# Last inverse transform step on four quarters of TensorE's array, with a radix-2 step over s1, in a kernel of a 2-D spectral filter and a dense MLP

## The chip, the cores and the metric

One core of a Trainium2 chip runs the kernel alone. The metric is device time in microseconds (us) of one execution; lower is better. The engines are TensorE (PE; its weight loads are PEld), VectorE (DVE), ScalarE (ACT), GpSimd (POOL) and SyncE (SP). SP does nothing here but issue DMAs, one after the other, from one queue.

## What is computed

The reference, cut to what matters; x is 2048 tokens of 512 numbers, F is 1792:

```python
def _A_ref(x, w_r, w_i):                 # spectral filter
    X = rfft2(x); X = X * (w_r + 1j * w_i)
    return irfft2(X, (S, D))
def _B_ref(x, w1, b1, w2):               # dense -> mish -> dense
    h = einsum("bsd,df->bsf", x, w1) + b1
    return einsum("bsf,fd->bsd", h * tanh(softplus(h)), w2)
xn = layernorm(x)
out = x + _A_ref(xn, w_r, w_i) + _B_ref(xn, w1, b1, w2)
```

## The kernel before

**Numbers.** Every f32 operand of a matmul is split into a high and a low f16 part, and each product is three matmuls: high x high, high x low, low x high. `mm3` (L85) does such a triple; its three calls are L88, L91 and L92.

**The MLP.** Tokens form four groups g of 512, F forms 14 slices f of 128. A *half tile* is either `mlp_up(g, f)` (L771; twelve matmuls into `ph`, then on ScalarE a Mish and on ScalarE and VectorE the split of its result into `a`) or `mlp_down(g, f)` (twelve matmuls into four accumulators `pa`). Both are 128x128 weights by 128x512. There are 112 half tiles; the generator `mlp_all` (L856) hands them out one by one, and `half_tile` takes the next. The tokens of a group lie as columns of `xnT[g]`; `turn` and `copies` (L328) fill it. At the end of a group `mlp_end` (L845) adds the accumulators onto the rows `macc`, which by then hold x plus the spectral part; only group 3 does it in the other order: the spectral part comes first, and `mlp_end` stores the result.

**The transforms.** The token number is 16 s1 + s2. Forward: over s1 (`s1_forward`), over s2 with a first step over d (`p2_unit`, tile `psP`), over d (`d_pair`, `psD`); the product with the filter (`spectrum`); back over d (`dp_unit`, `psA`), over s2 (`ip_unit`, `psT`), and over s1 (`s1_inverse`, L886, `psY`). Between the steps the data go through HBM to be turned: `d_y1`, `d_a` and `d_t`. So an `ip_unit` reads its rows `ai` from `d_a`, makes six matmuls, and its result goes over ScalarE (`bc_t`), VectorE (`bt_t`), ScalarE (the cast to `tt`) and GpSimd (the low part of `tt`) to `d_t`. `s1_inverse` reads `yi` from `d_t`, in 512-byte pieces, once all sixteen `ip_unit`s have stored. `p2_unit` runs pairs of matmuls that use half of the array's columns each, `d_pair` pairs that use half of its rows each.

**The order.** From L1122 on the spectral work (`stream_a`, 120.6 units of weight, N_WGT) is mixed with half tiles so that at its end `B_END` = 98 of the 112 are given out. Then sixteen `s1_inverse` calls, one for each s2, are spread over the remaining 14: call k comes (k + T_LAG)(112 - T_HOLD - 98)/16 half tiles later, the first after three, and two half tiles are kept for the end. A scheduler turns this into an order for each engine; it may move the matmuls of half tiles past those of `s1_inverse`, of which only the first of three is held in place.

```python
def s1_inverse(g, s):
    s2 = 4 * g + s
    yi = qp.tile([P, 4, 2, P], F16, tag="q1", name=f"yi_{s2}")       # 4 buffers, shared with ai and yt
    ...
    psf = ps_f.tile([P, D], F32, tag="f", name=f"psY_{s2}")          # 2 buffers, shared with psP ... psT
    ...
    nc.vector.scalar_tensor_tensor(m, psf, sc["k"], m, op0=ALU.mult, op1=ALU.add)
    nc.sync.dma_start(outv[:, s2, :], m)
```

Of the kernel before, what the change touches and what calls it, by code (L numbers as in the profile page):

```python
# [19 lines left out]
P = 128  # L20
NS2 = 16
# [10 lines left out]
B_END = 98  # L32
T_LAG = 4
T_HOLD = 2
# [7 lines left out]
def spectral_mlp_kernel(ctx, tc, x, wt, w0, w1, b1, w2, cT, cIT, cM, out):  # L42
# [16 lines left out]
    outv = out.rearrange("(p s) d -> p s d", s=NS2)  # L59
# [179 lines left out]

    def turn(pt, xh, h):  # L240
        for dc in range(4):
            nc.tensor.transpose(pt[:, h, dc, :], xh[:, h, dc * P : (dc + 1) * P], ident)
# [10 lines left out]
    def first_group(ts):  # L253

        pe, act, dve = mybir.EngineType.PE, mybir.EngineType.Activation, mybir.EngineType.DVE
        with in_order(pe, act, dve):
# [4 lines left out]
            xTv = xnT[0].rearrange("p h c (s t) -> p h c s t", s=4)  # L261
# [26 lines left out]
            def copy(s):  # L288
                nc.vector.tensor_copy(xTv[:, 0, :, s, :], pt[s][:, 0])
                return nc.scalar.copy(xTv[:, 1, :, s, :], pt[s][:, 1])  # L290
# [33 lines left out]
    def turned_rows(g, s, xh):  # L324
# [6 lines left out]
        def copies():  # L331
            xTv = xnT[g].rearrange("p h c (s t) -> p h c s t", s=4)
            nc.vector.tensor_copy(xTv[:, 0, :, s, :], pt[:, 0])
            nc.scalar.copy(xTv[:, 1, :, s, :], pt[:, 1])  # L334
# [409 lines left out]
    def ip_unit(c, g):  # L744
# [4 lines left out]
        for k in range(2):  # L749
# [12 lines left out]
        nc.sync.dma_start(  # L762
            d_t.rearrange("a (c f) e -> (a c) (f e)", c=2)[:, fg * 1024 : (fg + 1) * 1024],
            tt.rearrange("p l h e -> p (l h e)"),
        )
# [116 lines left out]
    def load_it():  # L882
        t = cp.tile([P, NS2, 2, P], F16, tag="cT", name="cITt")
# [3 lines left out]
    def s1_inverse(g, s):  # L887
        s2 = 4 * g + s
        yi = qp.tile([P, 4, 2, P], F16, tag="q1", name=f"yi_{s2}")
        nc.sync.dma_start(  # L890
            yi.rearrange("p a h e -> p a (h e)"),
            d_t[4 * s2 : 4 * s2 + 4].rearrange("a p e -> p a e"),
        )
        psf = ps_f.tile([P, D], F32, tag="f", name=f"psY_{s2}")
        yv = yi.rearrange("p a h (b e) -> p h b a e", b=2)
        mm3(
            psf.rearrange("p (b a e) -> p b a e", b=2, a=4),
            lambda h: sc["cIT"][:, s2, h, :],
            lambda h: yv[:, h],
            True,  # L900
            True,
            True,
        )
        if g < 3:
            m = macc[g][:, s, :]
            nc.vector.scalar_tensor_tensor(m, psf, sc["k"], m, op0=ALU.mult, op1=ALU.add)  # L906
# [373 lines left out]
```

## Time and profile before

| | |
|---|---|
| three runs | 400.53, 398.08, 399.92 us; median 399.92 |
| the profiled execution | 398.09 us, of which the trace spans 396.3 |
| TensorE busy | 379.8 us of the span, 2481 matmuls |
| VectorE, ScalarE, GpSimd busy | 241.2, 210.3, 68.9 us |
| DMA | 61.6 MB, mean 155 GB/s |
| granted TensorE clock | 1.00 |

The trace's times are microseconds from its start. A row of a group gives busy time in us, then the mean duration of one in ns. A matmul's duration contains its way through the array (a 128x512 one lasts 0.38 us), but one follows the other sooner; how fast matmuls go is read from the distance of their starts. In brackets stands how long an engine stood idle before an instruction, and what ended the wait.

### The profile page before, as it was taken

How to read it: one execution, taken by the hardware profiler on the slowest of the kernel's cores; microseconds unless marked ns; L12 is line 12 of the kernel's file. 1: busy time of each engine (PE TensorE's matmuls, PEld its weight loads, DVE VectorE, ACT ScalarE, POOL GpSimd, SP SyncE). 2: the span in 40 equal slices, each digit the busy share in tenths (PEclk: the TensorE clock that was granted, in tenths of full speed). 3: DMA queues.
4: the chain of work that ended last, by engine and by line, in shares of the span. 5: the costliest groups of instructions: out<-in, count | busy, mean ns of one | idle time of the engine just before them, and what ended most of it. 6: DMA issues, size and time to landing. Idle time of an engine off the chain costs nothing. (4 is left out here: it accounts for less than half of the span.)

```text
span 396.3 us, 6567 instructions
## 1 busy us (share of the span) xinstructions
PE 379.8 (96%) x2481; PEld 190.7 (48%) x2481; DVE 241.2 (61%) x505; ACT 210.3 (53%) x337; POOL 68.9 (17%) x100
## 2 busy tenths in 40 slices
PE   8799897999999999999999999999999999999995
PEld 3444343455544445456444565454655456444442
DVE  5789773465566724984597644957349972424334
ACT  3869858478665426564644555366455464423110
POOL 0000018366644400000021100121001120220000
PEclk9999999999999999999999999999999999999999
DMA  8995014335157894055732636226652022744556
GB/s 286 372 402 244 1 55 132 108 126 168 53 160 217 237 276 127 0 134 131 242 108 80 163 105 180 91 104 159 216 160 80 27 81 73 218 151 135 172 194 253
DMA packets 49519, 61.61 MB, mean 155 GB/s; under 512 B 3776, under 2 KB 36032, under 8 KB 48848
## 3 DMA queue, kind: packets, MB, share of 16 engines
q1 hardware_dynamic: 49488, 61.20, 49.1%
q8 instruction: 19, 0.31, 0.3%
q14 instruction: 12, 0.10, 0.1%
HBM read 44.38 MB, written 16.78 MB: 154 GB/s over the span
## 5 line engine op out<-in xcount | busy, mean ns | idle before, releaser
L781 PE MATMUL ph<-xnT,w1t 128*128 128x512 f16 x672 | 153.4, 379 | 1.3 <-ACT xnT L334 0.8
L781 PEld LDWEIGHTS <-w1t 128*128 128x128 f16 x672 | 65.0, 98 | 78.6 <-issue 1.5
L91 PE MATMUL pa<-w2r,a 128*128 128x512 f16 x224 | 84.9, 379 | 2.9 <-DVE w2r L499 1.9
L88 PE MATMUL pa<-w2r,a 128*128 128x512 f16 x224 | 85.0, 379 | 0.8 <-ACT w2r L496 0.5
L92 PE MATMUL pa<-w2r,a 128*128 128x512 f16 x224 | 84.9, 379 | 0.0
L795 ACT ACTIVATE hb<-ph,b1t,sc_exp 128x512 f32<-128x512 f32 x56 | 43.2, 772 | 56.1 <-PE ph L781 56.0
L816 DVE SCALAR_TENSOR_TENSOR a<-hb,sc_a,a 128x512 f16<-128x512 f32 x56 | 41.8, 750 | 51.0 <-ACT a L813 50.7
L133 POOL TENSOR_TENSOR tt<-bt_t,tt 128x512 f16<-128x512 f32 x16 | 19.9, 1245 | 186.3 <-ACT tt L132 186.3
L813 ACT ACTIVATE a<-hb,sc_a 128x512 f16<-128x512 f32 x56 | 40.1, 720 | 1.5
L92 PEld LDWEIGHTS <-a 128*128 128x128 f16 x224 | 21.9, 98 | 29.1 <-issue 3.7
L91 PEld LDWEIGHTS <-a 128*128 128x128 f16 x224 | 21.9, 98 | 25.5 <-issue 1.9
L88 PEld LDWEIGHTS <-a 128*128 128x128 f16 x224 | 21.9, 98 | 25.2 <-issue 0.8
L379 ACT ACTIVATE u<-r,sc_u 128x512 f16<-128x512 f32 x16 | 11.5, 720 | 23.6 <-DVE r L679 15.5
L133 POOL TENSOR_TENSOR y<-bt_s,y 128x512 f16<-128x512 f32 x16 | 18.7, 1177 | 10.8 <-issue 6.0
L132 ACT CAST tt<-bt_t 128x512 f16<-128x512 f32 x16 | 9.9, 616 | 15.9 <-DVE bt_t L128 12.5
L906 DVE SCALAR_TENSOR_TENSOR m<-psY,sc_k,m 128x512 f32<-128x512 f32 x12 | 8.7, 746 | 14.9 <-PE psY L92 14.9
L237 POOL TENSOR_TENSOR xh<-xs,xh 128x512 f16<-128x512 f32 x12 | 14.5, 1210 | 10.3 <-ACT xh L236 10.3
L734 DVE SCALAR_TENSOR_TENSOR at<-psA,at 128x512 f16<-128x512 f32 x16 | 10.7, 687 | 8.7 <-ACT at L733 8.7
L611 ACT ACTIVATE ix<-psD 64x512 f32<-64x512 f32 x16 | 9.5, 594 | 11.2 <-PE psD L599 10.9
L132 ACT CAST y<-bt_s 128x512 f16<-128x512 f32 x16 | 9.9, 616 | 10.4 <-DVE bt_s L128 7.6
L588 DVE SCALAR_TENSOR_TENSOR z<-psP,z 128x512 f16<-128x512 f32 x16 | 10.5, 684 | 7.8 <-ACT z L587 7.8
L127 DVE SCALAR_TENSOR_TENSOR bt_s<-psS,bc_s 128x256 f32<-128x256 f32 x16 | 6.7, 422 | 13.1 <-ACT bc_s L123 9.5
(158 smaller groups left out, 512.7 us busy)
## 6 DMA issues: line engine op xcount, KB each, us to landing
wt<-in_wt_dram SPq DMA_DIRECT2D x32, 256.0 KB
x<-in_x_dram SPq DMA_DIRECT2D x8, 512.0 KB
d_y<-y SPq DMA_DIRECT2D x16, 256.0 KB
wm<-in_wt_dram SPq DMA_DIRECT2D x8, 512.0 KB
yt<-d_y SPq DMA_DIRECT2D x16, 256.0 KB
d_a<-at SPq DMA_DIRECT2D x32, 128.0 KB
ai<-d_a SPq DMA_DIRECT2D x16, 256.0 KB
d_t<-tt SPq DMA_DIRECT2D x16, 256.0 KB
```

Of the source, the lines that this page charges most:

```text
L88: first = nc.tensor.matmul(ps, stat(0), mov(0), start=start, stop=False)
L91: nc.tensor.matmul(ps, stat(0), mov(1), start=False, stop=False)
L92: return nc.tensor.matmul(ps, stat(1), mov(0), start=False, stop=stop)
L132: nc.scalar.copy(out[:, :, 0, :], tv)
L133: nc.gpsimd.tensor_sub(out[:, :, 1, :], tv, out[:, :, 0, :])
L237: nc.gpsimd.tensor_sub(xh[:, 1, :], xs, xh[:, 0, :])
L379: hi = nc.scalar.activation(dst_h, src, AF.Copy, scale=scale)
L734: nc.vector.scalar_tensor_tensor(at[:, :, 1, :], psv, 2.0**-15, at[:, :, 0, :], op0=ALU.mult, op1=ALU.subtract)
L781: last_mm = nc.tensor.matmul(ph, w1t[:, hs, dc, f * P : (f + 1) * P], xnT[g][:, hm, dc, :], start=n == 0, stop=n == 11)
L795: nc.scalar.activation(hb, ph, AF.Mish, bias=b1t[:, f : f + 1], scale=s_exp[k])
L813: hi = nc.scalar.activation(a[:, 0, :], hb, AF.Copy, scale=sc["a"])
L816: lo = nc.vector.scalar_tensor_tensor(a[:, 1, :], hb, sc["a"], a[:, 0, :], op0=ALU.mult, op1=ALU.subtract)
```

## The change

The inverse over s1 is a sum over 64 frequencies f1, real and imaginary: 128 rows. Split by the parity of f1 (`be`), 64 rows each, the sum over even f1 is the same for s1 and s1 + 64, and that over odd f1 has the other sign. So for one s2 it is enough to compute 64 outputs t from the even rows and 64 from the odd rows, and then even + odd and even - odd. Each of these is a matmul of 64 rows by 64 columns of weights, a quarter of the array: row half by parity, column half (`i`) by which of two s2 of a pair. One call of the new `s1_inverse(g, q)` does two s2, 4g + q and 4g + 2 + q: twelve matmuls 64*64 by 512 into two PSUM tiles, even and odd, where two old calls made six 128*128 by 512.

What follows from it: the odd tile is copied by ScalarE (`odd`), VectorE does two multiply-adds from the even tile and one add, GpSimd one subtraction. Output rows now come as 64 t by i; so the columns of `xnT` are written in that order (`columns`), the residual rows are loaded and the results stored by 64 partitions, group 3's stores from SP's and ScalarE's queue. The rows of `d_t` are sorted by parity, so `tt` is stored by two DMAs. The turned rows of a pair are loaded one call ahead (`load_yi`); a call's stores are issued before the next call but after its loads. The order of TensorE in this stage is fixed as written (`in_order`). B_END is 97, T_LAG and T_HOLD are 3, and the last call is three half tiles before the end. The constants of this step (cIT) are half as large. The diff's core:

```diff
-B_END = 98
-T_LAG = 4
-T_HOLD = 2
+B_END = 97
+T_LAG = 3
+T_HOLD = 3
...
+    def columns(xT):
+        v = xT.rearrange("p h c (w q i t) -> p h c q i w t", w=2, q=2, i=2)
+        return [v[:, :, :, s % 2, s // 2] for s in range(4)]
...
         def copies():
-            xTv = xnT[g].rearrange("p h c (s t) -> p h c s t", s=4)
-            nc.vector.tensor_copy(xTv[:, 0, :, s, :], pt[:, 0])
-            nc.scalar.copy(xTv[:, 1, :, s, :], pt[:, 1])
+            xTv = columns(xnT[g])
+            pv = pt.rearrange("p h c (w t) -> p h c w t", w=2)
+            nc.vector.tensor_copy(xTv[s][:, 0], pv[:, 0])
+            nc.scalar.copy(xTv[s][:, 1], pv[:, 1])
...
-        nc.sync.dma_start(
-            d_t.rearrange("a (c f) e -> (a c) (f e)", c=2)[:, fg * 1024 : (fg + 1) * 1024],
-            tt.rearrange("p l h e -> p (l h e)"),
-        )
+        rows = d_t.rearrange("a (b c f) e -> b a c (f e)", b=2, c=2)
+        for be in range(2):
+            nc.sync.dma_start(
+                rows[be, :, :, fg * 512 : (fg + 1) * 512],
+                tt[:, 2 * be : 2 * be + 2].rearrange("p l h e -> p (l h e)"),
+            )
...
     def rows_back(g):
         macc[g] = cp.tile([P, 4, D], F32, tag=f"xnT{g}", name=f"m_{g}")
-        nc.sync.dma_start(macc[g], xv[:, 4 * g : 4 * g + 4, :])
+        for i in range(2):
+            nc.sync.dma_start(
+                macc[g][64 * i : 64 * i + 64].rearrange("t (w q) d -> t w q d", w=2),
+                xp[:, :, 4 * g + 2 * i : 4 * g + 2 * i + 2],
+            )
...
-                nc.sync.dma_start(outv[:, 4 * g + s, :], m[:, s, :])
+                for i, eng in enumerate((nc.sync, nc.scalar)):
+                    eng.dma_start(outp[:, s // 2, 4 * g + 2 * i + s % 2], m[64 * i : 64 * i + 64, s, :])
...
     def load_it():
-        t = cp.tile([P, NS2, 2, P], F16, tag="cT", name="cITt")
+        t = cp.tile([P, NS2, 2, 64], F16, tag="cT", name="cITt")
         nc.sync.dma_start(t, cIT.rearrange("p (s h q) -> p s h q", s=NS2, h=2))
         sc["cIT"] = t
-    def s1_inverse(g, s):
-        s2 = 4 * g + s
-        yi = qp.tile([P, 4, 2, P], F16, tag="q1", name=f"yi_{s2}")
-        nc.sync.dma_start(
-            yi.rearrange("p a h e -> p a (h e)"),
-            d_t[4 * s2 : 4 * s2 + 4].rearrange("a p e -> p a e"),
-        )
-        psf = ps_f.tile([P, D], F32, tag="f", name=f"psY_{s2}")
-        yv = yi.rearrange("p a h (b e) -> p h b a e", b=2)
-        mm3(
-            psf.rearrange("p (b a e) -> p b a e", b=2, a=4),
-            lambda h: sc["cIT"][:, s2, h, :],
-            lambda h: yv[:, h],
-            True,
-            True,
-            True,
-        )
+    def load_y(q):
+        y = sc["y", q] = big.tile([P, 2, D], F32, tag="big", name=f"y_{q}")
+        for i in range(2):
+            nc.sync.dma_start(y[64 * i : 64 * i + 64], xp[:, :, 12 + 2 * i + q])
+    yi_of, to_store = {}, []
+    def load_yi(g, q):
+        yis = []
+        for i in range(2):
+            s2 = 4 * g + 2 * i + q
+            yi = qp.tile([P, 4, 2, P], F16, tag="q1", name=f"yi_{s2}")
+            nc.sync.dma_start(
+                yi.rearrange("p a h e -> p a (h e)"),
+                d_t[4 * s2 : 4 * s2 + 4].rearrange("a p e -> p a e"),
+            )
+            yis.append(yi.rearrange("p a h (b e) -> p h b a e", b=2))
+        yi_of[g, q] = yis
+    def store_rows():
+        while to_store:
+            g, q = to_store.pop(0)
+            mv = macc[g].rearrange("p (w q) d -> p w q d", w=2)
+            for i in range(2):
+                nc.sync.dma_start(outp[:, :, 4 * g + 2 * i + q], mv[64 * i : 64 * i + 64, :, q])
+    def s1_inverse(g, q):
+        yis = yi_of.pop((g, q))
+        ps = [ps_f.tile([P, D], F32, tag="f", name=f"psY_{g}_{q}_{be}") for be in range(2)]
+        for t, (hs, hm) in enumerate(((0, 0), (0, 1), (1, 0))):
+            for i in range(2):
+                for be in (1, 0):
+                    rows = slice(64 * be, 64 * be + 64)
+                    mm = nc.tensor.matmul(
+                        ps[be][64 * i : 64 * i + 64].rearrange("p (b a e) -> p b a e", b=2, a=4),
+                        sc["cIT"][rows, 4 * g + 2 * i + q, hs, :],
+                        yis[i][rows, hm],
+                        start=t == 0,
+                        stop=t == 2,
+                    )
+                    tc.keep_in_program_order(mm)
+        odd = tp.tile([P, D], F32, tag="bt", name=f"odd_{g}_{q}", bufs=2)
+        nc.scalar.activation(odd, ps[1], AF.Copy, scale=sc["k"])
         if g < 3:
-            m = macc[g][:, s, :]
-            nc.vector.scalar_tensor_tensor(m, psf, sc["k"], m, op0=ALU.mult, op1=ALU.add)
-            nc.sync.dma_start(outv[:, s2, :], m)
+            ms = [macc[g][:, 2 * w + q, :] for w in range(2)]
         else:
-            if s % 2 == 0:
-                sc["y"] = big.tile([P, 2, D], F32, tag="big", name=f"y_{s2}")
-                nc.sync.dma_start(sc["y"], xv[:, s2 : s2 + 2, :])
-            y = sc["y"][:, s % 2, :]
-            nc.vector.scalar_tensor_tensor(y, psf, sc["k"], y, op0=ALU.mult, op1=ALU.add)
-            yacc.setdefault(g, []).append(y)
+            ms = [sc["y", q][:, w, :] for w in range(2)]
+            yacc.setdefault(g, {}).update({2 * w + q: ms[w] for w in range(2)})
+        for w in range(2):
+            nc.vector.scalar_tensor_tensor(ms[w], ps[0], sc["k"], ms[w], op0=ALU.mult, op1=ALU.add)
+        nc.vector.tensor_add(ms[0], ms[0], odd)
+        nc.gpsimd.tensor_sub(ms[1], ms[1], odd)
+        if g < 3:
+            to_store.append((g, q))
...
-    todo = [(3, s) for s in range(4)] + [(g, s) for g in range(3) for s in range(4)]
+    load_y(0)
+    load_y(1)
+    todo = [(3, q) for q in range(2)] + [(g, q) for g in range(3) for q in range(2)]
+    load_yi(*todo[0])
     start, n = done[0], len(todo)
     total = 2 * 4 * NFC
-    for k in range(n):
-        while done[0] - start < (k + T_LAG) * (total - T_HOLD - start) / n and half_tile():
+    with in_order(mybir.EngineType.PE):
+        for k in range(n):
+            while done[0] - start < T_LAG + k * (total - T_HOLD - T_LAG - start) / (n - 1) and half_tile():
+                pass
+            if k + 1 < n:
+                load_yi(*todo[1])
+            store_rows()
+            s1_inverse(*todo.pop(0))
+        store_rows()
+        while half_tile():
             pass
-        s1_inverse(*todo.pop(0))
...
-    order = (np.arange(2)[:, None] * 64 + np.arange(64).reshape(16, 2, 2).transpose(0, 2, 1).reshape(1, 64)).reshape(128)
-    IT = T.transpose(2, 1, 0)[order]
+    order = (np.arange(2).reshape(1, 2, 1, 1) * 64 + np.arange(64).reshape(16, 2, 2).transpose(2, 0, 1)[:, None]).reshape(128)
+    IT = T.transpose(2, 1, 0)[order][:, :, :64]
```

How the change moves instructions, at four places. In these rows L is the line in the file that the row is from; `ph_3_8` is `mlp_up` of group 3, slice 8, `pa` is `mlp_down`, `psT_15` the last `ip_unit`, and the number after that a tile's own. "..." leaves out the rest of such a group of matmuls and their weight loads.

TensorE, before, from the last `ip_unit` to the first last-step matmul (psY):

```order
L88 MATMUL psT_15_4117<-ai_15_4115,cMt_88 128x256
...
L88 MATMUL pa_3_3_3740<-w2r_93,a_3_5_3858 128x512
...
L781 MATMUL ph_3_9_4145<-xnT_3_1251,w1t_92 128x512
...
L88 MATMUL pa_3_0_3737<-w2r_93,a_3_6_3926 128x512
...
L781 MATMUL ph_3_10_4184<-xnT_3_1251,w1t_92 128x512
...
L88 MATMUL psY_12_4177<-yi_12_4175,cITt_1367 128x512
...
```

TensorE, after, the same place:

```order
L90 MATMUL psT_15_4117<-ai_15_4115,cMt_88 128x256
...
L792 MATMUL ph_3_8_4144<-xnT_3_1252,w1t_92 128x512
...
L90 MATMUL pa_3_0_3769<-w2r_93,a_3_5_3891 128x512
...
L792 MATMUL ph_3_9_4174<-xnT_3_1252,w1t_92 128x512
...
L939 MATMUL psY_3_0_1_4197<-yi_12_4140,cITt_1368 64x512
...
L939 MATMUL psY_3_0_0_4196<-yi_12_4140,cITt_1368 64x512
...
L939 MATMUL psY_3_0_1_4197<-yi_14_4142,cITt_1368 64x512
...
```

Between psT_15 and psY stood 3 + 12 + 12 + 8 = 35 full matmuls, now 5 + 12 + 12 = 29. The third psY matmul needs a second turned row, yi_14. At the end of the program TensorE's last work was six psY matmuls and is now 36 of `pa`.

ScalarE, before, in the last `ip_unit`s:

```order
L795 ACTIVATE hb_3_8_4110<-ph_3_8_4097,b1t_94,sc_exp_1_317 128x512
L813 ACTIVATE a_3_8_4112<-hb_3_8_4110,sc_a_327 128x512
L123 ACTIVATE bc_t_14_4089<-psT_14_4081 128x256
L132 CAST tt_14_4088<-bt_t_14_4091 128x4x128
L123 ACTIVATE bc_t_15_4125<-psT_15_4117 128x256
L132 CAST tt_15_4124<-bt_t_15_4127 128x4x128
```

ScalarE, after:

```order
L125 ACTIVATE bc_t_13_4075<-psT_13_4067 128x256
L125 ACTIVATE bc_t_14_4106<-psT_14_4098 128x256
L134 CAST tt_13_4074<-bt_t_13_4077 128x4x128
L134 CAST tt_14_4105<-bt_t_14_4108 128x4x128
L125 ACTIVATE bc_t_15_4125<-psT_15_4117 128x256
L806 ACTIVATE hb_3_8_4157<-ph_3_8_4144,b1t_94,sc_exp_1_317 128x512
L134 CAST tt_15_4124<-bt_t_15_4127 128x4x128
L824 ACTIVATE a_3_8_4159<-hb_3_8_4157,sc_a_327 128x512
```

The last unit's first copy now stands behind the casts of two other units, and hb_3_8 has moved ahead of its cast. On TensorE these units, too, stand closer: psT_13 and psT_14 without a matmul between them, three full ones before psT_15.

SP, after, the DMAs of the last four `ip_unit`s and the first `yi`:

```order
L748 DMA d_a_86<-at_13_3975 64x4x256 x2
L756 DMA ai_12_4046<-d_a_86 128x2x512
L748 DMA d_a_86<-at_14_4005 64x4x256 x2
L748 DMA d_a_86<-at_15_4023 64x4x256 x2
L756 DMA ai_13_4065<-d_a_86 128x2x512
L756 DMA ai_14_4096<-d_a_86 128x2x512
L756 DMA ai_15_4115<-d_a_86 128x2x512
L773 DMA d_t_87<-tt_12_4055 64x2x512 x2
L773 DMA d_t_87<-tt_13_4074 64x2x512 x2
L773 DMA d_t_87<-tt_14_4105 64x2x512 x2
L773 DMA d_t_87<-tt_15_4124 64x2x512 x2
L916 DMA yi_12_4140<-d_t_87 128x4x256
```

Before, ai_13 was issued ahead of the stores of at_14 and at_15, and ai_15 only after the store of tt_12. The first psT_12 has 14 full matmuls between it and the last psA, before it had ten.

In the spectral stream before that the new pace moves half tiles about: before the very first psT, 45 full matmuls follow the last psA (22 before), and at two places where twelve full matmuls stood between two pairs of psP units only two are left.

More of the change, by code (lines that the diff above doesn't have):

```diff
@@ L58, in spectral_mlp_kernel @@
     xv = x.rearrange("(p s) d -> p s d", s=NS2)
-    outv = out.rearrange("(p s) d -> p s d", s=NS2)
+    xp = x.rearrange("(w t s) d -> t w s d", w=2, s=NS2)
+    outp = out.rearrange("(w t s) d -> t w s d", w=2, s=NS2)
     d_y1 = dp.tile([64, P, 256], F16, tag="d_y1", name="d_y1")
@@ L260, in first_group @@
             xnT[0] = cp.tile([P, 2, 4, 512], F16, tag="xnT0", name="xnT_0")
-            xTv = xnT[0].rearrange("p h c (s t) -> p h c s t", s=4)
+            xTv = columns(xnT[0])
             def high(s):
@@ L288, in copy @@
             def copy(s):
[L289 to L290 removed]
+                pv = pt[s].rearrange("p h c (w t) -> p h c w t", w=2)
+                nc.vector.tensor_copy(xTv[s][:, 0], pv[:, 0])
+                return nc.scalar.copy(xTv[s][:, 1], pv[:, 1])
             qs = w1_norm(0, lambda: high(0))
```

3 lines of the change are left out of this document (1 added, 2 removed).

## Prediction

> **What bounds the kernel now.** I read the engine totals first, then the same totals by stage, then the chain that ended last, and at the end TensorE's own timeline around the waits.
>
> ```profile
> PE 379.8 (96%) x2481; PEld 190.7 (48%) x2481; DVE 241.2 (61%) x505; ACT 210.3 (53%) x337; POOL 68.9 (17%) x100
> ...
> 148.00:230.00 82.00, 79.80 (x690) 42.58 (x689) 57.41 (x132) 45.05 (x74) 5.13 (x4) 1.00 0.44 126
> 230.00:317.00 87.00, 86.84 (x667) 46.56 (x664) 56.75 (x126) 44.63 (x76) 7.52 (x6) 1.00 0.41 123
> ...
> 336.17:355.00 18.83, 17.90 (x95) 8.66 (x92) 6.38 (x13) 8.20 (x15) 4.63 (x4) 1.00 0.56 174
> 355.00:392.20 37.20, 37.14 (x172) 16.76 (x172) 16.09 (x23) 6.00 (x8) 0.00 (x0) 1.00 0.57 187
> ```
>
> The columns are stretch, length, busy time and count of PE, PEld, DVE, ACT, POOL, then granted clock, DMA share, GB/s. From 148 us on TensorE has no slack: 37.14 of 37.20 us in the last stage, and the clock is 1.00. A microsecond taken from TensorE there is one taken from the end, unless TensorE then waits. Where it waits already is between 336 and 355 us, and the chain says for what:
>
> ```profile
> 347.22 1.16 POOL tt L133
> ...
> 349.05 1.20 POOLq L1276
> ...
> 350.27 1.96 DMA d_t<-tt
> ...
> 352.31 2.62 DMA yi<-d_t
> ...
> 355.06 0.38 PE psY L88
> ...
> 360.61 2.59 PE ph L781 x12
> ```
>
> The last unit of the inverse over s2 leaves TensorE, passes ScalarE, VectorE and GpSimd, is written to HBM (1.96 us), read back turned (2.62 us), and only then can the last transform step begin. Twelve full matmuls take 2.59 us: 0.216 each.
>
> **The matmuls themselves.** Before: 48 of 128x512, so 48 x 0.216 = 10.4 us. After: 96 on a quarter of the array, twelve to a group, eight groups. Quarter-array matmuls are not in this trace, half-array ones are, in both directions:
>
> ```profile
> 146.00 2.54 PE L781 MATMUL ph<-xnT,w1t 128*128 128x512 f16 x11
> 148.46 1.53 PE L575 MATMUL psP<-cMt,yt 128*64 128x128 f16 x48
> 149.93 0.39 PE L781 MATMUL ph<-xnT,w1t 128*128 128x512 f16 x1
> ...
> 161.50 0.38 PE L92 MATMUL pa<-w2r,a 128*128 128x512 f16 x1
> 161.81 1.48 PE L599 MATMUL psD<-z,cMt 64*128 64x256 f16 x24
> 163.23 2.76 PE L781 MATMUL ph<-xnT,w1t 128*128 128x512 f16 x12
> ```
>
> Split by columns (psP): TensorE was due at 146.00 + 11 x 0.216 = 148.37 and was free for the next matmul at 149.93, so 48 matmuls of 128 columns cost 1.56 us. One after the other they would need 48 x 0.054 = 2.59, in pairs 1.29. Split by rows (psD): due at 161.72, free at 163.23, 1.51 us for 24 of 256 columns, against 2.59 singly and 1.29 in pairs. Each split alone halves the time, less 0.22 to 0.27 us for going in and out. I take both splits to multiply: a group is 3 x 0.216 + 0.25 = 0.90 us, eight are 7.2. **Term 1: 7.2 - 10.4 = -3.2 us.** The best end is 24 x 0.216 = 5.2 (-5.2); the worst I allow is that only two run at once, 10.4 + 8 x 0.25 = 12.4 (+2.0).
>
> Here a rule of the Trainium skill speaks against the change (TensorE: Matmul & The Clock Gate, Part 3: Packing small matmuls): a weight load overlaps running matmuls only if its row group is another one. By it the quadrants of one row half would take turns, and the step would cost the 12.4 us. The psP row does not bear it out: its two tiles use all 128 rows, so the row group is the same, and still a load and a matmul went in every 1.56/48 = 0.033 us. No run shows it for quadrants yet.
>
> **The first wait for turned rows.** Here the gain can be given back. The new code ends the previous stream one half tile earlier (B_END 97) and fixes TensorE's order.
>
> ```profile
> 346.23 0.27 PE L88 MATMUL psT<-ai,cMt 128*128 128x256 f16 x1 [0.15 <-DMA ai<-d_a]
> ...
> 355.06 0.38 PE L88 MATMUL psY<-yi,cITt 128*128 128x512 f16 x1 [0.46 <-DMA yi<-d_t]
> ...
> 347.08 0.38 ACT L123 ACTIVATE bc_t<-psT 128x256 f32<-128x256 f32 x1
> ...
> 348.39 0.62 ACT L132 CAST tt<-bt_t 128x512 f16<-128x512 f32 x1 [0.94 <-POOL tt L133]
> ...
> L762 SPq DMA_DIRECT2D d_t<-tt x16: 319/327/338, 199.9 to 350.3; - x16
> L890 SPq DMA_DIRECT2D yi<-d_t x16: 359/360/507, 352.3 to 384.6; - x16
> ...
> L795 ACT ACTIVATE hb<-ph,b1t,sc_exp 128x512 f32<-128x512 f32 x56 | 43.2, 772 | 56.1 <-PE ph L781 56.0
> ...
> 355.00:356.50 1.50, 1.44 (x7) 0.71 (x8) 0.60 (x1) 0.00 (x0) 0.00 (x0) 1.00 1.03 305
> ```
>
> From the last psT unit's start (346.23) to psY (355.06) the chain takes 8.83 us. TensorE covered all but 0.46 of it with the unit's own six matmuls (0.65) and 35 full ones. In the new order only 29 stand there: 0.65 + 29 x 0.216 = 6.9 us. The chain itself grows: ScalarE, which works in order, has the casts of two earlier units (0.62 each) ahead of the last bc_t, and an hb (0.77) ahead of the last cast; working these through, the last GpSimd subtraction ends 4.75 us after the unit's start instead of 4.02 (350.25 - 346.23), so +0.7. The store of tt is two issues, +0.33. The first group needs two turned rows; the second is issued 0.36 later, +0.4. Chain 8.83 + 0.7 + 0.33 + 0.4 = 10.3; wait 10.3 - 6.9 = 3.4. **Term 2: 3.4 - 0.46 = +2.9 us.** With none of the additions it would be 1.9 (+1.5); a second row late by a whole 0.86 us (256 KB at the 305 GB/s of the last row) makes it +3.4. Since TensorE is in order, all of pa, ph and the other seven groups stand behind this wait, and every store behind them.
>
> **Waits before it.** Three more rows:
>
> ```profile
> 195.25 0.20 PE L88 MATMUL psT<-ai,cMt 128*128 128x64 f16 x1 [0.80 <-DMA ai<-d_a]
> ...
> 214.37 1.48 PE L599 MATMUL psD<-z,cMt 64*128 64x256 f16 x23 [0.78 <-DVE bt_t L128]
> ...
> 338.87 0.28 PE L88 MATMUL psT<-ai,cMt 128*128 128x256 f16 x1 [0.37 <-DMA ai<-d_a]
> ```
>
> In the last four psT units, ai_15 is no longer behind a store of d_t on SP's queue, and the first has 14 full matmuls (3.0 us) ahead of it where ten (2.2) left it 0.37 short; by the issue times none waits. **Term 3: -0.37 - 0.15 = -0.5.** The spectral stream is reshuffled by B_END: before the first psT stand 23 more full matmuls, so its 0.80 goes; two psP pairs move to two matmuls apart, where their evictions make them wait about 0.25 each. **Term 4: -0.8 + 0.5 = -0.3**, with bounds -1.6 (both rows gone) and +1.5 (twice the longest one new).
>
> **The added eviction work, at nothing.** Per group one ScalarE copy, one VectorE add and one GpSimd subtraction are new; the PSUM multiply-adds stay sixteen.
>
> ```profile
> L133 POOL TENSOR_TENSOR tt<-bt_t,tt 128x512 f16<-128x512 f32 x16 | 19.9, 1245 | 186.3 <-ACT tt L132 186.3
> L906 DVE SCALAR_TENSOR_TENSOR m<-psY,sc_k,m 128x512 f32<-128x512 f32 x12 | 8.7, 746 | 14.9 <-PE psY L92 14.9
> L619 DVE TENSOR_TENSOR r<-r,t_c 128x512 f32<-128x512 f32 x8 | 5.5, 682 | 0.1
> L588 DVE SCALAR_TENSOR_TENSOR z<-psP,z 128x512 f16<-128x512 f32 x16 | 10.5, 684 | 7.8 <-ACT z L587 7.8
> L333 DVE COPY xnT<-pt 128x512 f16<-128x512 f16 x12 | 4.9, 411 | 5.7 <-PE pt L242 5.7
> ```
>
> The ScalarE copy reads PSUM as hb does (0.77). That is 8 x 0.77 = 6.2 us of ScalarE, 8 x 0.68 = 5.5 of VectorE, 8 x 1.25 = 10 of GpSimd, in a stage where they are busy 6.0, 16.1 and 0 of 37.2. The tight spot: a group takes both PSUM buffers, and four times only twelve matmuls (2.59) lie before the next. VectorE needs two multiply-adds and often an activation remainder between them, 3 x 0.75 = 2.25, plus 0.2 to start. It fits by 0.1; without that cover each place costs up to 0.5, 2 us in all. The xnT copies into 64-element runs, the split row loads, and SP's sixteen more tt issues (5.3 us over 190) lie under busy TensorE; only the first group's four VectorE copies lie on the path, and at the 0.68 of z's f16 write instead of 0.41 they would add 1.1. I take 0.
>
> **The end.**
>
> ```profile
> 388.50:390.00 1.50, 1.50 (x8) 0.69 (x7) 1.50 (x3) 0.00 (x0) 0.00 (x0) 1.00 0.00 0
> 390.00:392.20 2.20, 2.20 (x11) 0.88 (x9) 2.20 (x4) 0.00 (x0) 0.00 (x0) 1.00 0.95 362
> 392.20:394.93 2.73, 0.14 (x1) 0.00 (x0) 0.99 (x2) 0.00 (x0) 0.00 (x0) 1.00 1.00 378
> 394.93:396.30 1.37, 0.00 (x0) 0.00 (x0) 0.00 (x0) 0.00 (x0) 0.00 (x0) 1.00 0.01 5
> ```
>
> Seven stores (1.8 MB) fill the DMA engines from 390.0 to 394.9, yet the last, released at 393.2, lands only some 0.2 us later than alone. Now the down projection ends last: four multiply-adds of 0.75 behind matmuls 0.65 apart end about 1.1 us after TensorE, as today's (393.2 - 392.2 = 1.0), and four stores are left instead of seven. **Term 5: -0.1**, bounds -0.7 and +0.5.
>
> **Sum:** -3.2 + 2.9 - 0.5 - 0.3 - 0.1 = -1.2 us. The profiled execution took 398.09, so 396.9 for it; it lay 1.83 below the median 399.92, so **398.7** as a median.
>
> **Rivals.** *No wait at the first group:* the halves land sooner and the chain costs no more cover than it did; 398.7 - 2.9 = 395.8. For it: 0.46 today. Against: six matmuls of cover fewer. *The quadrants run two at a time:* mechanism and place are term 1's worst end, 398.7 + 5.2 = 403.9, slower than before; the change would not do what it says. It decides once a group takes over about 1.35 us (term 1 then adds 0.4 and the sum is +2.4). For it: nothing here shows four at once. Against: both halvings in the rows. *The long wait slows TensorE afterwards:* the kernel's first matmuls, after idleness, ran slower:
>
> ```profile
> 1.17 8.12 PE L251 MATMUL ps_warm<-warm 128*128 128x512 f16 x29 [1.17 <-DVE warm L246]
> ...
> 66.93 0.38 PE L91 MATMUL pa<-w2r,a 128*128 128x512 f16 x1 [1.94 <-DVE w2r L499]
> ```
>
> 28 steps took 8.12 - 0.38 = 7.74 us instead of 6.04, 1.7 lost; 398.7 + 1.7 = 400.4. The longest wait once the projections run is the 1.94 us of the second row, so a longer one is untested. The Trainium skill (TensorE: Matmul & The Clock Gate, Why this matters for your kernels) asks for no gaps over about 3 us, and a 3.4 us wait would break that.
>
> **Chances:** forecast 0.55, no wait 0.20, two at a time 0.12, slow again 0.13. The forecast's own range is 397 to 400.5. To keep four fifths I go down to 395.5 (no wait) and up to 402.5, leaving out most of two-at-a-time. One per cent, about what this kernel's measurement can tell from none, is 395.9 and 403.9: under it lie half of the no-wait case and a tail of the forecast (0.17), over it half of two-at-a-time and a tail (0.09), between them 0.74.
>
> **What would show it.** Right: psY groups of twelve in about 0.9 us; one wait of about 3 us for yi before the first, none at the other seven; psT without waits; three full pa groups at the end. Wrong: groups of 1.3 us or more; the first psY under 1 us late; waits on the evictions at the 12-matmul gaps; psP or psD waits in the stream that sum to over 2 us; copies into xnT over 0.5 us.

## The result, and the profile after

| | before | after |
|---|---|---|
| median of the runs | 400.02 us (398.08 to 400.53, 6 runs) | 406.01 us (404.25 to 406.99, 6 runs) |
| ratio, 95% interval | | 1.0169 [1.014, 1.0198] |
| the profiled execution, its span | 398.09, 396.3 us | 406.04, 404.2 us |
| last VectorE instruction to the end | 3.1 us | 4.5 us |

Slower by 6 us; the prediction was 398.7. The profiled executions differ by 7.9 us of span, more than the medians: that of the kernel before is the shortest of its six. The engine totals and the granted clock of the changed kernel, in 40 slices:

```profile
PE 381.2 (94%) x2529; PEld 189.1 (47%) x2529; DVE 247.8 (61%) x513; ACT 215.9 (53%) x345; POOL 80.9 (20%) x108
...
PEclk9999999999999999999999999999999999969999
```

TensorE is busy 1.4 us longer though it has less to do, and one slice, 354 to 364 us, has a lower clock. TensorE's timeline there and at the second group (start, length):

```profile
346.84 0.28 PE L90 MATMUL psT<-ai,cMt 128*128 128x256 f16 x1
...
357.20 2.12 PE L939 MATMUL psY<-yi,cITt 64*64 64x512 f16 x12 [3.27 <-DMA yi<-d_t]
359.26 0.61 PE L90 MATMUL pa<-w2r,a 128*128 128x512 f16 x1
359.66 0.63 PE L93 MATMUL pa<-w2r,a 128*128 128x512 f16 x1
...
363.74 2.75 PE L792 MATMUL ph<-xnT,w1t 128*128 128x512 f16 x12
366.43 0.84 PE L939 MATMUL psY<-yi,cITt 64*64 64x512 f16 x12
367.20 0.39 PE L90 MATMUL pa<-w2r,a 128*128 128x512 f16 x1
```

Three readings. The second group starts at 366.43 and the next work at 367.20: twelve quarter-array matmuls in 0.77 us, four at once. It starts 0.1 us after TensorE was due (363.74 + 12 x 0.216 = 366.33), as every group does that comes without a wait, so it costs 0.87 in all. The last psT unit starts at 346.84 and the first group at 357.20, a chain of 10.36 us, of which 3.27 are idle. And behind that wait the first group takes 2.06 us, and full matmuls start 0.40 to 0.43 us apart instead of 0.216.

The chain that ended last gives the end of that wait, to be read beside the prediction's rows for `d_t`, `yi` and `psY`:

```profile
352.03 2.13 DMA d_t<-tt
354.42 2.65 DMA yi<-d_t
357.84 1.49 PE psY L939 x10
```

Two matmuls of the group start at 357.20; the other ten, of which the first needs the second turned row, only 0.64 us later. So not all of the 2.06 us is the clock. The stretches of this place (the column behind the five engines is the granted clock):

```profile
355.00:356.00 1.00, 0.00 (x0) 0.00 (x0) 0.47 (x1) 0.50 (x1) 0.00 (x0) 1.00 0.39 115
356.00:357.20 1.20, 0.00 (x0) 0.03 (x1) 0.28 (x1) 0.00 (x0) 0.00 (x0) 0.62 1.08 323
357.20:358.00 0.80, 0.80 (x6) 0.29 (x10) 0.00 (x0) 0.00 (x0) 0.00 (x0) 0.50 0.90 261
...
362.50:363.50 1.00, 1.00 (x4) 0.37 (x3) 0.00 (x0) 0.00 (x0) 0.00 (x0) 0.70 0.00 0
363.50:365.00 1.50, 1.50 (x8) 0.69 (x7) 0.00 (x0) 0.00 (x0) 0.00 (x0) 1.00 0.00 0
```

TensorE stopped at about 353.9; some 2.4 us later the clock fell to half, and it came back at 363, some six us after work had resumed.

Where the time of the two profiles differs, I add up TensorE's matmuls at their undisturbed rate from 133 us on and call what the starts lie behind that sum the *lost time*:

| part | before | after | difference |
|---|---|---|---|
| work of the last transform step | 10.4 | 6.2 | -4.2 |
| lost up to the last psT unit | 7.27 | 10.84 | +3.6 |
| lost in the first wait for yi | 0.63 | 3.44 | +2.8 |
| lost in the first group until its second row is there | 0 | 0.64 | +0.6 |
| lost to the clock (0.65 in the group, 1.89 in the next twelve) | 0 | 2.54 | +2.5 |
| lost in the later groups | 0 | 1.05 | +1.0 |
| from TensorE's end to the end | 3.96 | 5.33 | +1.4 |

Before rounding they sum to 7.8 of the 7.9 us. Of the 1.05 in the later groups 0.7 is the late start, 0.1 in each of seven groups, and 0.3 a wait for the second row of the last. For the second line, waits in the stream that were not there before:

```profile
312.80 0.38 PE L90 MATMUL pa<-w2r,a 128*128 128x512 f16 x1 [1.02 <-DVE m L867]
314.78 0.38 PE L90 MATMUL pa<-w2r,a 128*128 128x512 f16 x1 [0.51 <-DVE m L867]
316.96 1.48 PE L608 MATMUL psD<-z,cMt 64*128 64x256 f16 x23 [0.50 <-DVE bt_t L130]
```

The accumulators of a finished group are held because VectorE has other work ahead of `mlp_end`. Just ahead of it stands a subtraction that takes 1.21 us, where the next one of the same shape takes 0.29; a subtraction of GpSimd runs at the same time:

```profile
310.36 1.15 POOL L135 TENSOR_TENSOR tt<-bt_t,tt 128x512 f16<-128x512 f32 x1 [6.68 <-ACT tt L134]
310.45 1.21 DVE L687 TENSOR_TENSOR r<-ra 64x128 f32<-64x128 f32 x1
```

That the one slows the other is not shown by a run here. On SP's queue, the rows of `d_t` (count: shortest, median, longest issue in ns, first and last start in us) answer to the two that the prediction showed of before:

```profile
L773 SPq DMA_DIRECT2D d_t<-tt x32: 518/594/1279, 203.4 to 352.0; - x32
L916 SPq DMA_DIRECT2D yi<-d_t x16: 359/480/1092, 354.4 to 386.4; - x16
```

A half of tt takes 0.594 us to issue where the whole took 0.327. So the sixteen units hold SP for 32 x 0.594 = 19 us instead of 5.2. The last stretches:

```profile
399.00:400.00 1.00, 0.00 (x0) 0.00 (x0) 0.73 (x2) 0.00 (x0) 0.00 (x0) 1.00 0.97 262
400.00:401.00 1.00, 0.00 (x0) 0.00 (x0) 0.00 (x0) 0.00 (x0) 0.00 (x0) 1.00 0.90 299
401.00:402.00 1.00, 0.00 (x0) 0.00 (x0) 0.00 (x0) 0.00 (x0) 0.00 (x0) 1.00 0.95 287
```

The last stores, each of 64 rows, move 287 to 299 GB/s with the DMA engines 0.90 to 0.95 busy; before, the last stores moved 378.

### The profile page after: what moved, and what is told of

Same layout as the page of the kernel before. It is cut to its first block, busy times and chain, and to the rows that moved or that the text cites. A ratio compares the mean times of both kernels' runs of the same rounds, so it can differ in the third digit from the quotient of the medians.

```text
span 404.2 us, 6757 instructions
## 1 busy us (share of the span) xinstructions
PE 381.2 (94%) x2529; PEld 189.1 (47%) x2529; DVE 247.8 (61%) x513; ACT 215.9 (53%) x345; POOL 80.9 (20%) x108
## 4 chain that ended last, share of the span: by engine, by line
PE 57%; DVE 16%; ACT 10%; DMA 8%; issue 4%; POOL 2%; SPq 1%; DVEq 0%; ACTq 0%; POOLq 0%
PE ph L792 20%; PE pa L90 8%; PE pa L94 8%; PE pa L93 8%; PE psD L608 3%; DMA ai<-d_a 2%; PE psP L584 2%; DMA d_a<-at 2%; DVE m L867 2%; PE psY L939 2%; ACT a L824 2%; ACT hb L806 2%; PE pt L249 1%; ACT w1t L388 1%; DVE st L211 1%
## 5 line engine op out<-in xcount | busy, mean ns | idle before, releaser
L792 PEld LDWEIGHTS <-w1t 128*128 128x128 f16 x672 | 64.0, 98 | 77.4 <-issue 2.9
L134 ACT CAST tt<-bt_t 128x512 f16<-128x512 f32 x16 | 9.9, 617 | 13.2 <-DVE bt_t L130 10.4
L239 POOL TENSOR_TENSOR xh<-xs,xh 128x512 f16<-128x512 f32 x12 | 14.4, 1205 | 10.3 <-ACT xh L238 10.3
L742 ACT ACTIVATE at<-psA 128x512 f16<-128x512 f32 x16 | 9.2, 590 | 12.6 <-issue 7.5
L596 ACT ACTIVATE z<-psP 128x512 f16<-128x512 f32 x16 | 9.4, 595 | 12.1 <-PE psP L584 11.7
L134 ACT CAST y<-bt_s 128x512 f16<-128x512 f32 x16 | 9.9, 616 | 10.4 <-DVE bt_s L130 7.6
```

The lines of the kernel that those rows point to most:

```text
L134: nc.scalar.copy(out[:, :, 0, :], tv)
L239: nc.gpsimd.tensor_sub(xh[:, 1, :], xs, xh[:, 0, :])
L792: last_mm = nc.tensor.matmul(ph, w1t[:, hs, dc, f * P : (f + 1) * P], xnT[g][:, hm, dc, :], start=n == 0, stop=n == 11)
```

## The experiments

Kernels of one group shared the runs of the kernel before on one chip: its median was 399.13 us in the first group (13 runs), 398.79 in the second (25), 398.68 in the third (31). Two theories at first. **A**: the wait and the slow clock behind it are the main loss. **B**/**C**: what the step needs beside the matmuls (the pace, the split DMAs, the evictions) takes the gain; from the second group on C is the narrower theory that SP's queue is what holds the loads back.

### First group: the wait, the clock, the pace

**e1**, the change with one more half tile of cover.

```diff
-T_LAG = 3
+T_LAG = 4
```

> The changed kernel with T_LAG 4, so that 41 full matmuls instead of 29 stand between the last psT and the first psY; the stream before is instruction for instruction the same. Theory A (the 3.3 us wait for yi drops TensorE's clock, and both are lost time): the wait falls to about 0.9 us, the clock stays at 1.00, 406.0 - 2.4 - 3.2 = 400.4 us. Rival B (the clock falls because of the quarter-array matmuls, not of the wait): the granted clock is still 0.5 for some 6 us after the first psY, 403.6 us.

Measured 403.18 us (402.68 to 404.48), ratio 1.0104 [1.0068, 1.014]. The first group:

```profile
359.05 0.40 PE L939 MATMUL psY<-yi,cITt 64*64 64x512 f16 x2 [0.62 <-DMA yi<-d_t]
359.71 0.83 PE L939 MATMUL psY<-yi,cITt 64*64 64x512 f16 x10 [0.26 <-DMA yi<-d_t]
```

Two short waits, one for each of the two turned rows, and the clock there stays at 1.00. By the two ratios the change gets 0.65% faster, 2.6 us where theory A expected 5.6, and 4 us are still missing: the wait and its clock are a large part and not all.

**e2**, the change with matmuls that keep TensorE busy through the wait.

```diff
+        if (g, q) == (3, 0):
+            for _ in range(14):
+                tc.keep_in_program_order(nc.tensor.matmul(ps[0], ident, w1t[:, 0, 0, 0:512], start=True, stop=True))
```

> The changed kernel with 14 useless full matmuls into the psY buffer ahead of the first group, 3.0 us of TensorE work that fills the wait and computes nothing. The rows arrive as late as before. Theory A: only the slow clock goes, so 406.0 - 3.2 = 402.8 us, with the first real psY matmul at the same time as before. Rival B: the clock still falls at the first group, 406 us.

Measured 405.24 us (404.39 to 406.62), ratio 1.0154 [1.0115, 1.0193]. The first group, the stretch from its start, and the one of the twelve full matmuls behind it:

```profile
357.79 0.40 PE L942 MATMUL psY<-yi,cITt 64*64 64x512 f16 x2 [0.26 <-DMA yi<-d_t]
358.46 0.83 PE L942 MATMUL psY<-yi,cITt 64*64 64x512 f16 x10 [0.27 <-DMA yi<-d_t]
359.23 0.39 PE L90 MATMUL pa<-w2r,a 128*128 128x512 f16 x1
```

```profile
357.00:359.20 2.20, 1.67 (x15) 0.45 (x13) 0.00 (x0) 0.00 (x0) 0.00 (x0) 1.00 0.94 267
359.20:361.80 2.60, 2.60 (x14) 1.19 (x13) 2.01 (x3) 0.69 (x1) 0.91 (x1) 1.00 0.91 264
```

The clock stays at 1.00. The group takes 1.44 us (357.79 to 359.23), 0.67 of them for its second row, and the twelve matmuls that took 4.48 us take 2.59. From the last psT unit to the end of those twelve it is 2.5 us less than in the change, the 2.54 of the table, with 3.0 us of useless matmuls in it. So the idle time was what lowered the clock: the same quarter-array matmuls run here at 1.00. The medians don't show these 2.5 us: the ratio fell only from 1.0169 to 1.0154, with intervals that overlap. Executions of one kernel spread by 2 us, and the clock dips at other places too (in the profile of e1, for one, behind a wait of 1.95 us at 67.9 us).

**e3**, the kernel before at the change's pace, and **e4**, the change at the pace of before.

```diff
-B_END = 98      (e3, in the kernel before)
+B_END = 97
...
-B_END = 97      (e4, in the changed kernel)
+B_END = 98
```

> The kernel before with B_END 97 and nothing else. Theory A (the new pace alone makes the spectral stream lose some 3.5 us more in waits): 400.0 + 3.5 - 0.5 (the first psY no longer waits) = 403 us. Rival C (the stream's loss comes from the split stores and loads and the xnT copies): 399.5 us.

> The changed kernel with B_END 98: the stream's order is the old one but for a few places, and 26 full matmuls stand before the first psY. Theory A: the stream regains about 3.5 us, the wait is some 3.5 us and the clock still falls, 402.8 us. Rival C: the stream loses as much as in the changed kernel, 406.5 us.

e3: 400.16 us (399.06 to 402.0), ratio 1.0027 [1.0005, 1.0049]. By the last psT unit TensorE has lost 9.47 us instead of 7.27, +2.2 from the pace alone (theory A had 3.5), though at other places than in the change: its longest waits are 0.86 us at 176.67, 0.74 at 189.58 and 0.89 at 196.78. In this kernel 0.6 comes back, since its first psY does not wait. e4: 406.07 us (404.12 to 406.24), ratio 1.0161 [1.0122, 1.0199]. The stream's loss is gone (6.88 us at the first of the last four psT units, 6.81 before), so in the changed kernel all of it comes with the pace. The median has not moved, though. The profiled execution is the shortest of the four (404.12, the others 406.01 to 406.24), and its span is 2.2 us below that of the change: 3.8 are regained in the stream, and 1.6 are lost again at the last psT unit. What more the other three lost is not profiled. The profile shows:

```profile
347.86 0.27 PE L90 MATMUL psT<-ai,cMt 128*128 128x256 f16 x1 [1.45 <-DMA ai<-d_a]
...
357.58 0.40 PE L939 MATMUL psY<-yi,cITt 64*64 64x512 f16 x2 [3.29 <-DMA yi<-d_t]
```

```profile
343.08 1.45 SPq L773 DMA_DIRECT2D d_t<-tt  x2
344.69 0.47 SPq L756 DMA_DIRECT2D ai<-d_a  x1
345.21 7.87 SPq L773 DMA_DIRECT2D d_t<-tt  x6
```

The second fence is SP's queue: the last ai is issued behind the two halves of a tt, which hold the queue for 1.45 us, and that unit waits 1.45.

### Second group: is it the cover or the queue?

**e5**, the change with the old pace and 51 full matmuls of cover.

```diff
-B_END = 97
-T_LAG = 3
+B_END = 98
+T_LAG = 5
```

> The changed kernel with B_END 98 and T_LAG 5: the old order of the stream and 51 full matmuls between the last psT unit and the first quarter-array group. Theory A (the wait for turned rows and the slow clock behind it were the main loss, and the quarter arrays' gain is real): against the run with B_END 98 alone the wait of 3.5 us and the 2.4 us of slow matmuls behind it go, so about 399.5 median where the kernel before has 399.1; the clock at the groups is 1.00. Theory B (the loss lies in the half-row DMAs and the added eviction work of the stage): the wait only moves to later groups and the time stays above 402.5.

Measured 404.86 us (404.7 to 405.89), ratio 1.0142 [1.0114, 1.0171]. Theory A falls: with all the cover it asked for the kernel is nearly as slow as without. The profiled execution is the longest of the four (405.89, the others 404.70 to 404.92).

```profile
349.69 0.27 PE L90 MATMUL psT<-ai,cMt 128*128 128x256 f16 x1 [2.49 <-DMA ai<-d_a]
...
384.59 0.83 PE L939 MATMUL psY<-yi,cITt 64*64 64x512 f16 x10 [0.47 <-DMA yi<-d_t]
387.51 0.40 PE L939 MATMUL psY<-yi,cITt 64*64 64x512 f16 x2 [2.09 <-DMA yi<-d_t]
```

The wait moved: 2.49 us for the last ai, again with a slow clock behind it, and 2.09 for the last yi. This form also brings the last two groups together without matmuls between them, so that the last loads stand right behind stores:

```profile
381.45 1.26 SPq L929 DMA_DIRECT2D out_dram<-m  x2
382.80 1.88 SPq L916 DMA_DIRECT2D yi<-d_t  x2
385.09 4.78 SPq L929 DMA_DIRECT2D out_dram<-m  x4
```

**e6**, which takes the same order of the stream and moves the halves of tt and the stores to GpSimd's queue.

```diff
-T_HOLD = 3
+T_HOLD = 2
...
-            nc.sync.dma_start(
+            nc.gpsimd.dma_start(
                 rows[be, :, :, fg * 512 : (fg + 1) * 512],
...
-                nc.sync.dma_start(outp[:, :, 4 * g + 2 * i + q], mv[64 * i : 64 * i + 64, :, q])
+                nc.gpsimd.dma_start(outp[:, :, 4 * g + 2 * i + q], mv[64 * i : 64 * i + 64, :, q])
```

> As the run with B_END 98 and T_LAG 5, with T_HOLD 2, and with the halves of tt and the stored output rows of groups 0 to 2 issued from GpSimd's queue in place of SP's. Theory C (SP's queue, in which each 64-row DMA takes about 0.6 us to issue, holds ai_15 and the later yi back by 1.4 and 0.5 to 1.0 us): the wait of psT_15 for ai goes, the later groups wait under 0.2 us, and the time is 2 us below that run, about 397.5. Rival: GpSimd issues more slowly and its subtractions come later, so psT and the first group wait as long as they did; the time is within 0.7 us of that run.

Measured 397.61 us (396.98 to 399.21), ratio 0.9961 [0.9939, 0.9984]: 7.2 us below e5 and faster than the kernel before. On GpSimd an issue is no cheaper:

```profile
L773 POOL DMA_DIRECT2D d_t<-tt x32: 617/617/917, 204.4 to 352.4; - x32
```

But no load is queued behind it there, while SP now holds only loads, and TensorE stands idle nowhere in the stage; only the first group takes 0.15 us longer than the others:

```profile
341.67 1.45 SPq L756 DMA_DIRECT2D ai<-d_a  x2
354.63 22.94 SPq L916 DMA_DIRECT2D yi<-d_t  x16
```

```profile
346.16 0.27 PE L90 MATMUL psT<-ai,cMt 128*128 128x256 f16 x1
...
357.92 0.99 PE L939 MATMUL psY<-yi,cITt 64*64 64x512 f16 x12
```

e6 differs from e5 in T_HOLD as well, which separates the last two groups; by the two profiles the ai wait with its clock is some 4 us of the gain, the last groups are 4.4, and the slow matmuls behind these 0.8, of which the longer end takes back 2.1. What the queue did at the last two groups and what T_HOLD did there, no run takes apart. The lost time at the start of the last `pa` is 7.51 us, less than the 7.90 of before, so the quarter arrays bring their 4.2 us, less the late starts; the end gives most of it back, with 6.5 us from the last VectorE instruction to the end.

**e7** and **e8**, the kernel before with one thing of the change each: tt stored in two pieces, and the last four stores made by 64 rows.

```diff
+        rows = d_t.rearrange("a (c f) e -> a c (f e)", c=2)
+        for be in range(2):
+            nc.sync.dma_start(
+                rows[:, :, fg * 1024 + 512 * be : fg * 1024 + 512 * be + 512],
+                tt[:, 2 * be : 2 * be + 2].rearrange("p l h e -> p (l h e)"),
+            )
...
-                nc.sync.dma_start(outv[:, 4 * g + s, :], m[:, s, :])
+                for i, eng in enumerate((nc.sync, nc.scalar)):
+                    eng.dma_start(outv[64 * i : 64 * i + 64, 4 * g + s, :], m[64 * i : 64 * i + 64, s, :])
```

> The kernel before with one thing of the change: each tt is stored by two DMAs of 64x2x512 instead of one. Theory C (dear issues on SP): 32 issues of about 0.6 us instead of 16 of 0.33 put ai_15 and the last store later, psT_15 and the first psY wait 1 to 2 us more, about 400.6 where the kernel before has 399.1. Rival (the prediction's view: the issues lie under busy TensorE): within 0.5 us of it.

> The kernel before with one thing of the change: the last four stores are made by 64 rows, from SP's and ScalarE's queue. If the half-row stores are what makes the end longer (4.5 us from the last VectorE instruction to the end in every changed kernel, 3.1 before), the end grows by 1.0 to 1.4 us, about 400.3 median where the kernel before has 399.1. Rival (the end is longer because the stores come together behind the last multiply-adds): the end stays at 3.1 to 3.4 us and the time within 0.4 us of the kernel before.

e7: 402.01 us (400.1 to 403.02), ratio 1.0063 [1.004, 1.0087]. The issues and the two waits:

```profile
L764 SPq DMA_DIRECT2D d_t<-tt x32: 319/417/1497, 201.6 to 354.2; - x32
```

```profile
349.75 0.27 PE L88 MATMUL psT<-ai,cMt 128*128 128x256 f16 x1 [0.95 <-ACT tt L132]
358.86 0.38 PE L88 MATMUL psY<-yi,cITt 128*128 128x512 f16 x1 [0.74 <-DMA yi<-d_t]
```

An issue has a median of 0.417 us, less than in the change, whose rows are sorted by parity. The last ai stands behind two of them: it is issued at 346.72, 3.0 us before its unit starts, and the 0.95 us are the wait for it (the row names ScalarE's cast, which ends at that time too). The lost time before the first psY grows from 7.90 to 9.80. The stores that the prediction had at nothing cost about 2 us even in a kernel with nothing else changed. e8: 401.11 us (399.91 to 403.23), ratio 1.005 [1.0024, 1.0076]; from the last VectorE instruction to the end it takes 4.9 us, as the stretches of the end show:

```profile
396.00:397.00 1.00, 0.00 (x0) 0.00 (x0) 0.53 (x1) 0.00 (x0) 0.00 (x0) 1.00 0.93 299
397.00:398.00 1.00, 0.00 (x0) 0.00 (x0) 0.00 (x0) 0.00 (x0) 0.00 (x0) 1.00 0.95 309
398.00:399.00 1.00, 0.00 (x0) 0.00 (x0) 0.00 (x0) 0.00 (x0) 0.00 (x0) 0.55 1.01 365
```

299 to 365 GB/s where whole rows moved 378: so the split stores are the cause of the longer end. Every kernel here with whole-row stores has 3.1 to 3.2 us there, every one with 64-row stores 4.3 or more. The Trainium skill (SBUF — State Buffer, Door 1: The DMA port swizzle) says that partitions 0 to 63 reach only half of SBUF's ports, as 64 to 127 do. The rates are lower, as that would have it, but far above half of 378, and no run separates ports from the second queue, ScalarE's, that e8 uses as well.

### Third group: what remains

**e9** is e6 with the output rows back on SP's queue; **e10** issues each call's stores one call later from there, and the last tt from SP; **e11** is e10 with T_LAG 4 and T_HOLD 3; **e12** is the kernel before with its tt stores on GpSimd's queue.

```diff
-                nc.gpsimd.dma_start(outp[:, :, 4 * g + 2 * i + q], mv[64 * i : 64 * i + 64, :, q])
+                nc.sync.dma_start(outp[:, :, 4 * g + 2 * i + q], mv[64 * i : 64 * i + 64, :, q])
...
+            (nc.sync if fg == 15 else nc.gpsimd).dma_start(        (e10)
...
+            store_rows(1 if k + 2 < n else 0)        (e10: one call stays in the list)
...
-T_LAG = 5        (e11)
-T_HOLD = 2
+T_LAG = 4
+T_HOLD = 3
```

> As the run with both moved to GpSimd's queue, but only the halves of tt go there; the output rows of groups 0 to 2 are stored from SP's queue as in the change. Theory C splits the gain: ai and the first group wait no more (psT_15 under 0.4 us, first psY none), but the stores, which wait for GpSimd's subtraction on SP's queue ahead of the next yi, still hold up the later groups by 0.3 to 1 us each where nothing else does; the hardware-issued stores shorten the end by about 1 us against 6.6. About 398.5. Rival: the tt halves alone were the trouble, no waits at the later groups: 396.7.

> As the run before it, and each call's stores are issued one call later (never ahead of a yi that is needed sooner), and the last tt goes from SP's queue, which is idle then. Theory C: no wait of over 0.3 us at any group, the end 4.5 to 5.5 us after the last VectorE instruction, about 396.3. Rival: half-row stores pile up at the end and it stays at 6.6 us: 397.6.

> As the run with the stores deferred, with T_LAG 4 and T_HOLD 3: 39 full matmuls (9.1 us with the last psT unit) in place of 51 cover the chain of about 10.5 us, and 36 in place of 24 pa matmuls lie behind the last group. Theory D (a wait under 2 us costs itself, and the clock only falls behind longer ones): first psY waits about 1.5 us at clock 1.00, the end is 1 to 2 us shorter, within 0.7 us of the run with T_LAG 5. Rival: the clock falls behind the 1.5 us as well, and 2 to 3 us more are lost, about 399.

> The kernel before with its sixteen tt stores on GpSimd's queue, to see whether the queue alone brings a gain. SP holds only 0.34 us an issue there, so Theory C expects little: psT_15's 0.3 us goes, and the first psY waits about 0.9 us longer behind a slower store; 399.3 where the kernel before has 398.8. Rival: SP's queue already held the kernel before up, and it gains 1 us or more.

e9: 398.37 us (397.59 to 399.98, and one execution of 1010.8 that the ratio leaves out), ratio 0.9988 [0.9966, 1.001]. psT_15 doesn't wait, and the first group only for its second row (0.4 us); the last two groups lose 0.89 and 0.28 us behind the stores. e10: 397.61 (396.8 to 398.84), 0.997 [0.9952, 0.9987]: these two losses are gone (the first group takes 0.5 us for its second row), but the end stays at 6.5 us, against the expectation; it is as fast as e6. e11: 398.19 (397.17 to 399.88), 0.9989 [0.9968, 1.001]; the end is 4.7 us, and the shorter cover costs a wait, behind which the clock holds at 1.00 (the row names ScalarE; the first yi, issued at 353.55, arrives at about that time):

```profile
356.23 0.40 PE L939 MATMUL psY<-yi,cITt 64*64 64x512 f16 x2 [1.66 <-ACT a L824]
...
357.65 0.39 PE L90 MATMUL pa<-w2r,a 128*128 128x512 f16 x1
357.88 0.38 PE L93 MATMUL pa<-w2r,a 128*128 128x512 f16 x1
```

e12: 400.92 (398.99 to 401.47), 1.0038 [1.0017, 1.0058]: the slower path over GpSimd makes the first psY wait 1.44 us and gains nothing. So in the kernel before the move of the queue is no gain; in the changed one it lets through the gain of the quarter arrays. Open: why the end takes 5.9 to 6.5 us in e6, e9 and e10, with two half tiles behind the last group; stores of group 2 then still overlap the last ones, which no run here took apart.

## Why the prediction was wrong

On the profiled executions the forecast was -1.2 us and the result +7.8, so 9.0 are to be accounted for: 4.4 in terms 3 and 4, 2.5 by the clock, 1.5 at the end, 0.5 in the first wait, 0.3 in the last group, less 0.2 in the matmuls.

- **Term 1, the matmuls: right.** Counted as the prediction counted, from when TensorE was due, a group costs 0.87 us instead of 0.90: -3.4 instead of -3.2 (the table's -4.2 leaves out the late start of each group). Both splits multiply: four quarters run at once. The rival with two quadrants at a time did not come true, and the rule on row groups from the Trainium skill (TensorE: Matmul & The Clock Gate, Part 3: Packing small matmuls) did not hold for these quadrants.
- **Term 2, the first wait: right in kind, 0.5 short.** The first row is there after 10.36 us, the second after 11.0, where the forecast had 10.3 for both: +3.4 instead of +2.9. The turn over ScalarE (GpSimd's subtraction ends 4.59 us after the unit's start, forecast 4.75), the dearer store and the second row were the right additions. Too small were the store (its second half is issued 0.60 us behind that subtraction, forecast 0.33) and the second row (0.64, forecast 0.4).
- **The clock behind it: a rival that came true.** It had a chance of 0.13 and a price of 1.7, from the start of the kernel; it cost 2.5, as the clock stayed low for some six us of work. A wait of over 3 us was forecast in the likeliest case, so its effect on the clock belonged into the sum.
- **Term 3, psT without waits: half right.** A wait of 0.6 for ai stayed at the first of the last four psT units; psT_15 had none.
- **Term 4, the reshuffled stream: the largest step that failed, in size and sign.** Terms 3 and 4 together were to bring -0.8; they cost +3.6, and the upper bound of term 4 was +1.5. The wait of 0.80 went, as forecast, and the two psP places were found in the order. But the text priced only the places that it had found, and the new pace makes TensorE wait elsewhere: 2.0 us from 312 to 317, where VectorE comes late with tiles that TensorE needs, and 0.7 at 280.9 for a load. With the old pace the changed kernel has none of this loss (e4); in the kernel before the pace alone costs 2.2 (e3). Why it meets VectorE just there stays open.
- **The added work at nothing: the second step that failed.** The text said of SP's sixteen more tt issues that they "lie under busy TensorE", and priced each at the 0.327 us of a whole tt. Each half takes 0.594, and SP's queue is in order: what stands behind is the next ai and the next yi. In the kernel before the split alone makes 1.9 us of waits (e7). In the changed kernel at the old pace psT_15 waits 1.45 (e4) and 2.49 (e5) behind them, and not at all with the halves on another queue (e6). At the new pace SP has issued all four ai ahead of these stores, so in the change itself the step cost less than this: 0.3 in the store of term 2, and at most 0.3 at the last group, whose rows are loaded behind two stores of output rows. The term should have been read as a queue, not as busy time. The evidence was in the trace of before, in the 64-row stores of d_a:

```profile
338.27 2.60 SPq L739 DMA_DIRECT2D d_a<-at  x4
```

  That is 0.65 us each. The arithmetic of the engines held: GpSimd's subtraction took 1.58 us instead of 1.25, VectorE's multiply-adds 0.75, the copies into xnT 0.41 as before, and no group waited for an eviction. Seven groups were to be free of waits; six are, and the last waits 0.3 for its second row.
- **Term 5, the end: wrong.** -0.1 against +1.4. The number of stores was counted, their shape not: split by 64 rows they move 287 to 299 GB/s, and the same split makes the end of the kernel before 1.8 us longer (e8).

## What to carry to other kernels

An added DMA on an in-order queue is to be costed as a delay of the loads that are queued behind it, with the issue time of its own shape, and not as busy time that hides under the bottleneck. A long wait in front of TensorE can count nearly twice, once itself and once as the clock behind it: here waits of 2.1 to 3.3 us cost another 1.5 to 2.5 each (the change, e4, e5). A new pace of an interleaved stream is to be checked at every place where an accumulator is handed over, and not only where the order visibly changed. A smaller matmul bill is worth what it says only when the chains that feed it have a queue and a cover of their own; here it took four edits (pace, lag, hold, queue) to turn +1.7% into -0.4%.

## What the runs showed of the hardware

- Twelve 64x64 quadrant matmuls of 512 columns take 0.77 us to the start of the next matmul, and start 0.1 late: 0.87 in all, where three full ones are 0.65.
- Idle TensorE: behind 1.44 us (e12), 1.66 (e11) and 1.94 (the kernel before, at 66.93 us) the clock held at 1.00; behind 1.95 (e1, at 67.91), 2.09 and 2.49 (e5) and 3.3 (the change, e4) it fell to 0.50, and matmuls ran at half rate for some 3 to 6 us. With 14 matmuls in the gap (e2) it held. So the runs give no one length at which it falls.
- A DMA of a part can cost more to issue than one of the whole: on SP 0.594 us for half of tt's columns, sorted by parity, against 0.327 for a whole tt, and 0.478 for a last store of 64 rows against 0.332 for one of 128. GpSimd takes 0.617 for such a half of tt and 0.557 for a whole one.
